# Five x tiles turned by DMA transpose in a transformer block kernel, with weight rows moved and some weight lows on VectorE

## The chip, the core and the metric

The kernel runs on one NeuronCore of a Trainium2 chip. The metric is the device time in microseconds of one execution. The core has TensorE (PE, with its weight loads as PEld), VectorE (DVE), ScalarE (ACT), GpSimd (POOL) and the queue of SyncE (SP), from which nearly all DMAs of this kernel are issued. Each engine works through its own instructions in program order, and waits on semaphores for the others.

## What is computed

One pre-norm block on x of 2048 x 512, in float32: a layer norm, a sliding and dilated attention of 32 heads (8 positions, every second one), an output product with a residual, a second layer norm, and a dense part with squared relu.

```python
x = A_x
h = x + _A_ref(_layernorm(x), A_wqkv, A_wo)     # qkv, local attention, wo
h2 = h + _B_ref(_layernorm(h), B_w1, B_b1, B_w2, B_b2)
# _B_ref: r = relu(x @ w1 + b1); (r * r) @ w2 + b2
```

Float32 precision is kept on TensorE by writing each operand as a sum of a high part (a rounded float32r copy) and a low part (the rest), and by three matmul passes: high by high, low by high, high by low.

## The kernel before

The 2048 rows are 16 tiles of 128 rows. The instruction order of every engine is written out by hand: the program goes through numbered slots, and chores are hung on a slot. At the end of a slot (`end_slot`), the list `due` is run first (`at`), then the attention stream is pumped until its counted VectorE time (`now["dve"]`) has reached the counted TensorE time (`now["pe"]`), then the list `late` is run (`after`). So a chore given to `at` stands ahead of the slot's attention work in the queues of all engines, and one given to `after` stands behind it.

- **Opening** (lines 977 to 1002): 16 slots `n`, qkv products of tiles 0 to 3 by four column groups. Products go in turn to four PSUM banks.
- **First phases** (`first_phase(t0)`, lines 1007 to 1049, for t0 = 4, 6, ..., 14): each does the qkv products of tiles t0 and t0+1, three each, taken in turn (tile t0 first, then t0+1). There are 12 half slots `m`, two to a product; the slot ends in the middle of a product and after it. `evac` (ScalarE, line 523) of a product stands one slot after its end, so that of a phase's last product stands in the `due` list of slot m = 0 of the next phase, ahead of that slot's own chores. In slot 0 and in slot 2 come the statistics (`x_stats`, from tile 6 on ScalarE: `act_stats`, lines 182 to 184, with a finish on POOL) of tiles t0+2 and t0+3, then their norms (`x_norm`), and at m = 9 and 11 (7 and 8 where t0 is 12) their turns `x_T` on TensorE: four transposes into PSUM, a high part by ScalarE, a low part by VectorE (`lo_T`, in `late`). The product takes its passes in the order high by high, xh by the weights' low part, and xl last, so that xh is needed at its start and xl after two thirds of it.
- **Weight jobs** (`weight_job`, line 570): a row of `wo` or `w1` is loaded, and five slots later split: high on ScalarE, low on POOL. Twenty jobs go at m = 0, 3, 6, 9 of the phases 4 to 12.
- **Dense part**: four groups `u` of four tiles. While u = 0 runs (its body is at lines 1087 to 1162), the attention stream is still under way, and the 14 rows of `w2` are split (`split_w2`), low parts on POOL.
- **Attention stream**: multiplications and reductions on VectorE (lines 339, 350, 373) from windows loaded by SP (`load_window`, line 247, two buffers for k and two for v), and three additions on POOL for each step (line 407).
- **A turn by DMA** is already there for twelve o tiles and eight h tiles: `turn_split` (line 616, ScalarE) writes a tile as two planes of 16-bit halves, `turn_dma` (line 620) issues a DMA transpose from SP, and `turn_join` (line 625, ScalarE) puts the halves together again.

All row buffers (x tiles, their parts, raw weights, planes, h) come in rotation from one pool of 15.

Of the kernel before, what the change touches and what calls it, by code (L numbers as in the profile page):

```python
# [9 lines left out]
F32R = mybir.dt.float32r  # L10
# [6 lines left out]
P = 128  # L17
KB = D // P
FB = F // P
R = 4  # L20
# [15 lines left out]
SLOW = 1.01, 1.08, 1.05  # L36
DELAY = 3
WJ = 2
XT = (9, 11), (7, 8)
OT = 4, 5, 10, 12  # L40
WO = 7, 9, 13, 15
HT = 20, 20, 21, 23
# [10 lines left out]
HOLD = 1.0  # L53
XS = 6
WARM = 18


@with_exitstack
def block_kernel(ctx, tc, x, wqkv, wo, w1, b1, w2, b2, out):
    nc = tc.nc  # L60
# [39 lines left out]
    w2_h, w2_l = {}, {}  # L100

    def row(name, shape=(P, D), dt=F32):
        return work.tile(list(shape), dt, name=name, tag="row", bufs=ROWS)
# [9 lines left out]
    def at(delta, fn, *a):  # L113
        due.setdefault(now["slot"] + delta, []).append((fn, a))

    def after(delta, fn, *a):
        late.setdefault(now["slot"] + delta, []).append((fn, a))
# [18 lines left out]
    def dve(t):  # L136
        now["dve"] += t
# [13 lines left out]
    def hi(dst, src):  # L151
        nc.scalar.copy(dst, src)  # L152
# [45 lines left out]
    def transposes(src, banks="tr"):  # L198
        tr = turn[banks].tile("tr").rearrange("p (k c) -> p k c", k=KB)
        for k in range(KB):  # L200
            nc.tensor.transpose(tr[:, k, :], src[:, k * P:(k + 1) * P], ident)  # L201
        now["pe"] += 0.44
        return tr

    def parts(tr, dst):
        n = len(dst)
        return [(dst[i], tr[:, i * KB // n:(i + 1) * KB // n]) for i in range(n)]

    def hi_T(tr, h_dst):
        for d, src in parts(tr, h_dst):  # L210
            hi(d, src)
# [220 lines left out]
    xt, xT = {}, {}  # L432
# [35 lines left out]
    def x_T(t):  # L468
        tr = transposes(xt.pop(t))
        xT[t] = row("xh", (P, KB, P), F32R), row("xl", (P, KB, P), F32R)  # L470
        at(0, hi_T, tr, [xT[t][0]])
        after(0, lo_T, tr, [xT[t][0]], [xT[t][1]])

    ny = [0]

    turn["mm"] = Turn("mm0", "mm1", "acc0", "acc1")
# [63 lines left out]
    def qkv(t, gp, mid=None):  # L540

        ps = turn["mm"].tile("mm")
        xh, xl = xT[t]
        mm3(ps[:, :3 * GP], lambda k: xh[:, k, :], lambda k: xl[:, k, :],
            lambda k: pair(wq_h, k, gp), lambda k: pair(wq_l, k, gp), mid, lows_last=t > 0)
        at(1, evac, t, gp, None, ps)
# [20 lines left out]
    jobs = [(wo_h, wo_l, wo, k, 0, D) for k in range(KB)]  # L567
    jobs += [(w1_h, w1_l, w1, k, c * 448, 448) for k in range(KB) for c in range(4)]

    def weight_job():  # L570
        h, l, src, k, c0, cn = jobs.pop(0)
        raw = row("raw")
        nc.sync.dma_start(raw[:, :cn], src[k * P:(k + 1) * P, c0:c0 + cn])

        def split():
            hi(h[:, k, c0:c0 + cn], raw[:, :cn])
            after(0, lo, nc.gpsimd, l[:, k, c0:c0 + cn], raw[:, :cn], h[:, k, c0:c0 + cn])
        at(5, split)


    hs, hn = {}, {}
# [23 lines left out]
    planes = {}  # L605

    def halves_of(a):
        return a.bitcast(U16).rearrange("p (n two) -> p two n", two=2)

    def two_planes(a):  # L610
        return a.bitcast(U16).rearrange("p (two n) -> p two n", two=2)

    def turn_split(key, src):

        planes[key] = src, row("pl")
        nc.scalar.copy(two_planes(planes[key][1]), halves_of(src))
# [6 lines left out]
    def turn_join(key):  # L623
        src, pl = planes[key]
        nc.scalar.copy(halves_of(pl).rearrange("p two n -> p n two"),
                       two_planes(src).rearrange("p two n -> p n two"))
        planes[key] = pl.rearrange("p (k c) -> p k c", k=KB)
# [317 lines left out]
    warm = turn["tr"].tile("tr").rearrange("p (k c) -> p k c", k=KB)  # L945
    for n in range(WARM):
        nc.tensor.transpose(warm[:, n % KB, :], ident, ident)

    def start_T(t):
        x_T(t)  # L950
        run(due)
        run(late)
# [24 lines left out]
    for n in range(16):  # L977
        gp, t = divmod(n, 4)
        qkv(t, gp, (lambda: start_T(t + 1)) if n < 3 else None)
        if n == 0:  # L980
            x_rstd(2)
            x_center(3)
        if n == 1:
            x_rstd(3)
        if n < 6:
            for k in (0, 1):
                at(0, hi_wqkv, n // 2 + 1, n % 2 * 2 + k)
                after(0, lo_wqkv, n // 2 + 1, n % 2 * 2 + k,
                      nc.gpsimd if k or n < 2 else nc.vector)
        if n == 1:  # L990
            load_wqkv(3)
        if n == 13:
            consts()
        if n in (5, 6, 12, 14):
            at(0, load_x, n - 1 if n < 7 else n // 2)
        if n in (8, 9):
            at(0, x_stats, n - 4)
        if n in (11, 12):
            at(0, x_norm, n - 7)
        if n in (13, 14):  # L1000
            x_T(n - 9)
        end_slot(2.09)
# [4 lines left out]
    def first_phase(t0):  # L1007
        def chores(m):
            if t0 + 3 < 16:
                if m in (0, 2):  # L1010
                    at(0, x_stats, t0 + 2 + m // 2)

                early = t0 == 12
                if m + early in ((4, 6) if t0 == R else (6, 7)):
                    at(0, x_norm, t0 + 2 + (m + early) // 7 if t0 > R else t0 + m // 2)
                if m in XT[early]:
                    x_T(t0 + 2 + XT[early].index(m))
            if t0 + 5 < 16 and m in (6, 9):
                at(0, load_x, t0 + 2 + m // 3)
            if jobs and m % 3 == 0:  # L1020
                at(0, weight_job)
            k = t0 // 2 * 12 - 72 + m
            if k == 19:
                dve(HOLD)
            for t in range(R):
                if k == OT[t]:
                    at(0, load_h, t)
                    o_T(t)
                if t in HV and k == HK[t][0]:
                    at(0, h_split, t)  # L1030
                    after(0, turn_dma, ("h", t))
                if t in HV and k == HK[t][1]:
                    at(0, turn_join, ("h", t))
                if k == WO[t]:
                    wo_product(t, (1, 3, 4, 6))
                    now["pe"] += 2.73
                if k == HT[t]:
                    (at(0, h_parts, t) if t in HV else h_T(t))
            if k in W2:
                at(0, load_w2, W2.index(k))  # L1040

        def half(m):
            end_slot(1.37)
            chores(m)

        for n in range(6):
            chores(2 * n)
            qkv_of(t0 + n % 2, n // 2, lambda: half(2 * n + 1))
            end_slot(1.37)
# [19 lines left out]
    def split_w2(f):  # L1069
        raw = raws.pop(f)  # L1070
        hi(w2_h[f], raw)
        if f < 12:
            place[f] = free.pop(0)
            w2_l[f] = big_l[:, place[f]]
            at(1, stash, f)
        after(0, lo, nc.gpsimd, w2_l[f], raw, w2_h[f])

    def stash(f):
        nc.sync.dma_start(w2l_d[f], w2_l[f].bitcast(F32))
# [7 lines left out]
    for u in range(R - 1):  # L1087
# [11 lines left out]
        for i in js:  # L1099
            t = R * (u + 1) + i  # L1100
# [32 lines left out]
        for p in range(FB + LAG):  # L1133
# [17 lines left out]
            if q >= 0:  # L1151
                f = fs[q]
# [93 lines left out]
```

## Time and profile before

| | us |
|---|---|
| median of 3 runs | 510.53 (510.51 to 511.3) |
| profiled execution, its time | 510.24 |
| its span | 508.5 |

The profile is of one execution. Its times are microseconds from the span's start. In a timeline row stand the start, the duration, the engine, the line, the operation, what it writes and reads, and in brackets the idle time of that engine before it with what ended it. In a row of a group stand the busy time in all, the mean in ns of one, and the idle time before. The starts of the phases on TensorE are at 43.68 (t0 = 4), 61.76 (6), 79.64 (8), 96.92 (10), 114.21 (12) and 138.76 (14); u = 0 runs from 161.60 to about 254.

### The profile page before, as it was taken

Reading aid. Unit: us, or ns where it says so; the run is one execution under the profiler, and the core shown is the slowest. Engines: PE = TensorE matmul, PEld = TensorE weight load, DVE = VectorE, ACT = ScalarE, POOL = GpSimd, SP = SyncE. Lnnn points to the kernel's source line nnn. Section 1 sums busy time; section 2 is a strip of 40 time slices with the busy share of each in tenths; the row PEclk is TensorE's granted clock in tenths of the full one; section 3 lists DMA queues with packets and bytes.
Section 4 is the critical chain, followed back from the end, with each engine's and each line's share of the span. In section 5 each row is a group of like instructions: output and inputs, shape, how many; then the busy total and the mean of one; then the engine's idle time right before and its main releaser. Section 6 shows DMA issues by size and latency. Waiting matters only on the chain.

```text
span 508.5 us, 7542 instructions
## 1 busy us (share of the span) xinstructions
PE 498.6 (98%) x2422; PEld 420.5 (83%) x2422; DVE 375.2 (74%) x507; ACT 305.3 (60%) x558; POOL 361.4 (71%) x439
## 2 busy tenths in 40 slices
PE   8999999999999999999899999999999999999997
PEld 7998778888888887787688888888888888998986
DVE  6479899999999778986898989988951137732233
ACT  4635687577447747478454548756457847566541
POOL 5714789895776999989959777977896364685610
PEclk9999999999999999999999999999999999999999
DMA  8678889899698799789576756997572272444212
GB/s 271 189 212 204 245 290 302 245 307 303 201 228 253 253 273 278 215 216 291 166 248 207 216 147 165 257 252 244 161 173 63 80 212 83 169 123 144 64 43 83
DMA packets 109359, 102.61 MB, mean 202 GB/s; under 512 B 29448, under 2 KB 77832, under 8 KB 109320
## 3 DMA queue, kind: packets, MB, share of 16 engines
q1 hardware_dynamic: 108376, 101.61, 68.0%
q10 hardware_dynamic: 944, 0.52, 0.3%
q8 instruction: 19, 0.31, 0.2%
q14 instruction: 20, 0.16, 0.1%
HBM read 72.65 MB, written 24.25 MB: 191 GB/s over the span
## 4 chain that ended last, share of the span: by engine, by line
PE 66%; POOL 14%; DVE 2%; issue 2%; DMA 2%; ACT 1%; SPq 0%; POOLq 0%; ACTq 0%; DVEq 0%
PE mm L228 30%; PE acc L895 22%; PE wo L228 6%; PE mm L818 6%; POOL pr L407 5%; POOL rl L155 3%; POOL big_l L155 3%; PE tr L201 2%; POOL h L674 1%; DVE pr L350 1%; DMA q<-qkv_d 1%; DMA k<-qkv_d 1%; POOL o L407 1%; POOL w_x L155 1%; POOL rs L171 0%
## 5 line engine op out<-in xcount | busy, mean ns | idle before, releaser
L407 POOL TENSOR_TENSOR pr<-pr 128x512 f32<-128x512 f32 (+1 forms) x128 | 132.3, 1034 | 38.2 <-DVE pr L350 32.7
L228 PE MATMUL mm<-big_l,w_h 128*128 128x512 f32 x336 | 88.9, 391 | 0.7 <-ACT r L871 0.7
L350 DVE TENSOR_TENSOR pr<-ex,v 128x1024 f32<-128x1024 f32 x64 | 78.1, 1221 | 13.5 <-POOL o L407 10.1
L339 DVE TENSOR_TENSOR pr<-qp,k 128x1024 f32<-128x1024 f32 x64 | 76.8, 1200 | 9.3 <-ACT qp L268 8.4
L373 DVE TENSOR_REDUCE ex<-pr 128x64 f32<-128x1024 f32 x64 | 78.5, 1227 | 2.0
L228 PEld LDWEIGHTS mm<-big_l,w_h 128*128 128x128 f32 x336 | 62.8, 188 | 15.0 <-ACT r L871 2.0
L155 POOL TENSOR_TENSOR rl<-r,rh 128x512 fp32r<-128x512 f32 x42 | 55.6, 1326 | 14.9 <-ACT rh L152 14.9
L228 PE MATMUL mm<-big_l,xh 128*128 128x512 f32 (+1 forms) x208 | 55.8, 378 | 0.0
L228 PE MATMUL mm<-big_h,xh 128*128 128x512 f32 (+1 forms) x208 | 53.8, 379 | 1.3 <-ACT xh L152 1.3
L228 PE MATMUL mm<-big_h,xl 128*128 128x512 f32 (+1 forms) x208 | 52.7, 375 | 0.1
L895 PE MATMUL acc<-big_l,rh 128*128 128x512 f32 x190 | 52.2, 390 | 0.0
L895 PE MATMUL acc<-big_h,rh 128*128 128x512 f32 x190 | 52.1, 391 | 0.0
L895 PE MATMUL acc<-big_h,rl 128*128 128x512 f32 x190 | 51.7, 389 | 0.0
L871 ACT ACTIVATE r<-mm,b_sb 128x512 f32<-128x512 f32 x42 | 28.8, 685 | 33.6 <-PE mm L228 30.3
L228 PE MATMUL mm<-big_l,w_l 128*128 128x512 f32 x168 | 44.9, 389 | 0.0
L228 PEld LDWEIGHTS mm<-big_h,xh 128*128 128x128 f32 x208 | 37.6, 188 | 8.6 <-ACT xh L152 3.0
L228 PEld LDWEIGHTS mm<-big_h,xl 128*128 128x128 f32 x208 | 38.2, 188 | 6.4 <-DVE xl L155 0.5
L895 PEld LDWEIGHTS acc<-big_h,rl 128*128 128x128 f32 x190 | 35.7, 188 | 7.4
L895 PEld LDWEIGHTS acc<-big_l,rh 128*128 128x128 f32 x190 | 35.5, 188 | 7.4
L228 PEld LDWEIGHTS mm<-big_l,xh 128*128 128x128 f32 x208 | 37.5, 188 | 4.9
L895 PEld LDWEIGHTS acc<-big_h,rh 128*128 128x128 f32 x190 | 34.9, 188 | 6.7
L228 PEld LDWEIGHTS mm<-big_l,w_l 128*128 128x128 f32 x168 | 31.5, 188 | 6.6
(165 smaller groups left out, 917.8 us busy)
## 6 DMA issues: line engine op xcount, KB each, us to landing
k<-qkv_d SPq DMA_DIRECT2D x48, 288.0 KB, 3.1
v<-qkv_d SPq DMA_DIRECT2D x48, 288.0 KB, 3.6
qkv_d<-y SPq DMA_DIRECT2D x18, 512.0 KB, 5.1
big_l<-w2l_d SPq DMA_DIRECT2D x24, 256.0 KB, 3.1
xt<-in_A_x_dram SPq DMA_DIRECT2D x16, 256.0 KB, 4.7
q<-qkv_d SPq DMA_DIRECT2D x32, 128.0 KB, 3.7
h<-in_A_x_dram SPq DMA_DIRECT2D x16, 256.0 KB, 3.3
h_d<-h SPq DMA_DIRECT2D x16, 256.0 KB, 3.8
```

What stands on the lines that cost most here:

```text
L155: eng.tensor_tensor(out=dst, in0=src, in1=h, op=ALU.subtract)
L201: nc.tensor.transpose(tr[:, k, :], src[:, k * P:(k + 1) * P], ident)
L228: nc.tensor.matmul(ps, l(k), r(k), start=(n == 0), stop=(n == 3 * KB - 1))
L339: nc.vector.tensor_tensor(out=pr.rearrange("p i w h d -> p i w (h d)"), in0=qps["now"][:, j % 2].unsqueeze(2).to_broadcast([P, RI, W, GC]) ...
L350: nc.vector.tensor_tensor(out=p2, in1=vwin, op=ALU.mult, in0=e1[:, :, :, j * GH:(j + 1) * GH].unsqueeze(4).to_broadcast([P, RI, W, GH, DH]))
L373: nc.vector.tensor_reduce(out=lf[:, :, :, j * GH:(j + 1) * GH], in_=pr, axis=X, op=ALU.add)
L407: nc.gpsimd.tensor_tensor(out=dst, in0=p2[:, :, :w], in1=p2[:, :, w:2 * w], op=ALU.add)
L674: nc.gpsimd.tensor_tensor(out=h, in0=h, in1=b2_sb, op=ALU.add)
L818: nc.tensor.matmul(ps, sta[y][:, k], mov[x][:, k], start=(first and q == 0), stop=(last and q == len(terms) - 1), skip_group_check=True)
L871: nc.scalar.activation(r, ps, AF.Relu, bias=b1_sb[:, f:f + 1])
L895: nc.tensor.matmul(acc[j], l[:, j * P:(j + 1) * P], w[f], start=(first and n < len(js)), stop=(last and n >= len(terms) - len(js)))
```

## The change

1. In each phase with t0 up to 12 only the even tile t0+2 is turned on TensorE. The odd tile t0+3 (tiles 7, 9, 11, 13, 15) is split into planes in slot m = 8 (7 where t0 is 12), its DMA transpose stands in that slot's `late` list, and its join with the high and the low part (`x_join`) stands in the `due` list of slot m = 0 of the next phase, behind the statistics of that slot; for tile 15 in slot 11 of phase 12.
2. Weight jobs: three stand in the opening (n = 4, 6, 8), three in each phase up to 12 (m = 0, 4, 8), and the last two in phase 14 (m = 0 and 3). Their splits stand in `late`, four slots on for those of the opening and five for the others, and no longer in `due`.
3. The lows of the second weights' rows 1, 4, 7, 10 and 13 are made by VectorE in place of POOL, with 0.8 us each in the count that paces the attention stream.

```diff
-XT = (9, 11), (7, 8)
+XT = (9,), (7,)
+JOBS = 4, 6, 8
+JM = 0, 4, 8
...
+    def x_split(t):
+        turn_split(("x", t), xt.pop(t))
+
+    def x_join(t):
+        turn_join(("x", t))
+        tr = planes.pop(("x", t))
+        xT[t] = row("xh", (P, KB, P), F32R), row("xl", (P, KB, P), F32R)
+        hi_T(tr, [xT[t][0]])
+        after(0, lo_T, tr, [xT[t][0]], [xT[t][1]])
...
-    def weight_job():
+    def weight_job(delay=5):
...
-        at(5, split)
+        after(delay, split)
...
+        if n in JOBS:
+            at(0, weight_job, 4)
...
-                    x_T(t0 + 2 + XT[early].index(m))
+                    x_T(t0 + 2)
+                if m == 8 - early:
+                    at(0, x_split, t0 + 3)
+                    after(0, turn_dma, ("x", t0 + 3))
+            if m == 0 and R < t0 < 14:
+                at(0, x_join, t0 + 1)
+            if m == 11 and t0 == 12:
+                at(0, x_join, 15)
...
-            if jobs and m % 3 == 0:
+            if jobs and m in (JM if t0 < 14 else (0, 3, 5)):
...
-        after(0, lo, nc.gpsimd, w2_l[f], raw, w2_h[f])
+        eng = nc.vector if f % 3 == 1 else nc.gpsimd
+        after(0, lo, eng, w2_l[f], raw, w2_h[f])
+        if eng is nc.vector:
+            dve(0.8)
```

## The prediction

> **What bounds the kernel now.** Read first the page's busy shares, then who made TensorE wait, then the busy times by stage (each window, its length, then PE, PEld, DVE, ACT and POOL busy, the granted clock, the DMA share).
>
> ```profile
> span 508.5 us, 7542 instructions
> PE 498.6 (98%) x2422; PEld 420.5 (83%) x2422; DVE 375.2 (74%) x507; ACT 305.3 (60%) x558; POOL 361.4 (71%) x439
> ...
> PE tr L201 <- ACT hn L196: 1.4, 1, 1.4
> ...
> PE mm L228 <- ACT xh L152: 1.3, 2, 0.7
> PE wo L228 <- DVE ol L155: 0.8, 1, 0.8
> PE mm L228 <- ACT r L871: 0.7, 1, 0.7
> ...
> 96.00:113.00 17.00, 17.00 (x80) 14.10 (x79) 16.34 (x23) 11.65 (x27) 14.84 (x21) 1.00 0.92 276
> ...
> 164.00:190.00 26.00, 26.00 (x117) 21.52 (x116) 20.04 (x22) 16.02 (x27) 24.89 (x26) 1.00 0.81 254
> ...
> 215.00:240.00 25.00, 24.20 (x104) 19.29 (x104) 19.74 (x25) 19.45 (x29) 22.57 (x27) 1.00 0.93 240
> 240.00:255.00 15.00, 13.55 (x63) 10.76 (x62) 13.17 (x21) 7.73 (x17) 13.67 (x17) 1.00 0.62 187
> ```
>
> TensorE has hardly an idle moment: in the first phases (96 to 113) it is busy throughout, so whatever is taken from it or makes it wait there goes straight into the time. The waits of 0.8, 0.7 and 1.4 us (on `ol`, `r` and `hn`, all between 200 and 254) lie in the first group of the dense part. There POOL is busy 24.89 of 26 us and 13.67 of 15, and the wait for `hn` comes down from POOL's statistics:
>
> ```profile
> 251.07 0.61 POOL rs L171
> ...
> 252.08 0.82 ACT hn L196
> ```
>
> So two stages matter: TensorE sets the pace up to 161 us, and from there to 254 POOL's backlog costs it 0.8 + 0.7 + 1.4 = 2.9 us.
>
> **The turns taken from TensorE.** In the timeline of PE, a product without a turn and one with a turn in it:
>
> ```profile
> 96.92 1.09 PE L228 MATMUL mm<-big_h,xh 128*128 128x512 f32 x4
> ...
> 99.66 1.07 PE L228 MATMUL mm<-big_h,xh 128*128 128x512 f32 x4
> ...
> 107.82 1.07 PE L228 MATMUL mm<-big_h,xh 128*128 128x512 f32 x4
> 108.73 0.62 PE L228 MATMUL mm<-big_l,xh 128*128 128x512 f32 x2
> 109.19 0.60 PE L201 MATMUL tr<-ident,xt 128*128 128x128 f32 x4
> ...
> 111.02 1.07 PE L228 MATMUL mm<-big_h,xh 128*128 128x512 f32 x4
> ```
>
> A product takes 99.66 - 96.92 = 2.74 us, one with four transposes 111.02 - 107.82 = 3.20. A turn costs 0.46 us, and five fewer give 5 x 0.46 = **-2.3 us**. Nothing covers TensorE here, so all of it counts.
>
> **The splits at slot ends.** TensorE, ScalarE and the end of phase 4:
>
> ```profile
> 60.07 1.09 PE L228 MATMUL mm<-big_h,xl 128*128 128x512 f32 x4
> 61.76 1.20 PE L228 MATMUL mm<-big_h,xh 128*128 128x512 f32 x4 [0.60 <-ACT xh L152]
> 62.80 1.08 PE L228 MATMUL mm<-big_l,xh 128*128 128x512 f32 x4
> ...
> 64.00 1.20 PE L228 MATMUL mm<-big_h,xl 128*128 128x512 f32 x4
> ...
> 60.12 0.62 ACT L152 CAST wo_h<-raw 128x512 fp32r<-128x512 f32 x1 [2.35 <-DMA raw<-in_A_wo_dram]
> ```
>
> Four matmuls follow one another in 108.73 - 107.82 = 0.91 us. The last four of phase 4 would free the array at 60.98, and phase 6 starts at 61.76; its xl matmuls start at 64.00 where 62.80 + 0.91 = 63.71 was possible. That is 0.78 + 0.29 = 1.07 us lost, because ScalarE waited 2.35 us for a raw weight row ahead of the high part of tile 6. With the split in `late` and the jobs at other slots, that high part stands ahead of the wait: **-1.1 us** (0 if the raw row is late at another place).
>
> **The joins.** This is the term that decides. The odd tile is needed by the second product of a phase, 2.74 us after the phase's start. Its join stands in ScalarE's queue behind the evacuation of the last product of the phase before, which cannot start until that product is done, and behind a whole set of ScalarE statistics. Both are in the trace at the start of phase 10 (96.92), and a join with its high part, from an o tile, below them:
>
> ```profile
> 97.18 0.59 ACT L523 COPY y<-mm 128x512 f32<-128x512 f32 x1 [0.74 <-PE mm L228]
> ...
> 99.28 0.19 ACT L184 ACTIVATION_READ_ACCUMULATOR scrap<-xt,nm 128x1 f32 x1
> ...
> 237.78 1.16 ACT L625 COPY pl<-o 128x1024 uint16<-128x1024 uint16 x1
> 238.97 0.62 ACT L152 CAST oh<-pl 128x512 fp32r<-128x512 f32 x1
> ```
>
> The statistics end at 99.28 + 0.19 = 99.47. The join takes 238.97 - 237.78 = 1.19 to its reader's start, the high part 0.62: 101.28. The product could have started at 99.66. TensorE, in order, waits 1.6 us with nothing else to do, in each of the phases 6, 8, 10 and 12: 4 x 1.6 = **+6.4 us**. Tile 15, joined a slot before its phase, has time. The low part on VectorE stands behind the high part; xl is needed 2 x 0.91 us into the product, more than the 0.84 us of such a subtraction (row further down), so it adds nothing unless VectorE is late itself.
>
> The join also needs its DMA. What the trace says of such transposes, of a load for comparison (the last number is its median time to landing), of a transpose that was waited for, and of the place in SP's queue:
>
> ```profile
> L620 SPq DMA_TRANSPOSE o<-pl x12: 1237/1238/4488, 195.4 to 392.4; - x12
> DMA to landing us min/median/max: 3.5/6.3/7.0
> ...
> k<-qkv_d SPq DMA_DIRECT2D x48, 288.0 KB, 3.1
> ...
> 202.34 1.24 SPq L620 DMA_TRANSPOSE o<-pl  x1
> ...
> 205.98 1.18 ACT L625 COPY pl<-o 128x1024 uint16<-128x1024 uint16 x1 [0.90 <-DMA o<-pl]
> ...
> 59.42 1.16 DVE L339 TENSOR_TENSOR pr<-qp,k 128x1024 f32<-128x1024 f32 x1
> ...
> 61.71 0.53 SPq L247 DMA_DIRECT2D k<-qkv_d  x1
> ...
> 78.16 0.49 SPq L438 DMA_DIRECT2D xt<-in_A_x_dram  x1
> ```
>
> From issue to landing: 205.98 - 202.34 = 3.6 us where the join waited, 3.5 to 7.0 in the recorded ones. With the DMA share of 0.92 in phase 10 I take 4.5, nearer to the low end, where the wait was seen. In phase 4 the transpose stands behind the k load of 61.71, which overwrites a window that VectorE reads until 59.42 + 1.16 = 60.58. With 0.5 us for that load it issues at 61.1 and lands at 65.6; join and high part end at 65.6 + 1.8 = 67.4. The product would start at 60.98 - 0.46 + 2.74 = 63.3: a wait of 4.1 us, 2.5 over the 1.6. VectorE may be a little earlier with fewer loads queued, so I take **+2.0 us** (0 if VectorE and SP run 2 us earlier; 61.1 + 7.0 + 1.8 gives 69.9 and 5.0). In phase 6 the transpose stands just ahead of the load at 78.16; phase 8 would then start near 60.5 + 16.8 + 3.6 = 80.9 (six products of 2.74 and one turn are 16.9), and a landing at 82.7 lies ahead of the statistics' end 2.55 us after the start: 0, at worst (7.0) 1.7. Later phases start 1.6 us later each while VectorE, whose loads SP waits for, keeps its pace: 0.
>
> [...]
>
> **The lows on VectorE, and POOL's relief.**
>
> ```profile
> L155 POOL TENSOR_TENSOR big_l<-raw,big_h 128x512 fp32r<-128x512 f32 x12 | 15.6, 1298 | 0.0
> L155 DVE TENSOR_TENSOR rl<-r,rh 128x512 fp32r<-128x512 f32 x14 | 11.7, 836 | 22.5 <-ACT rh L152 21.2 <-POOL traw L788 1.4
> ```
>
> POOL loses 5 x 1.30 = 6.5 us in a stage in which it cost TensorE 2.9; VectorE gets 5 x 0.84 = 4.2 us where it has 26 - 20.04 = 6 us free from 164 to 190. TensorE also arrives later, so the attention stream has more of its work behind it. I take **-2.7 us** of the 2.9. The other end: the low waits on VectorE for ScalarE's high part, and the stream queued behind it (its multiplications, and POOL's additions after them) waits too; then 0, or a loss of about 1 us.
>
> **The three rows in the opening.** The highs of two of them (0.62 us each, as at 60.12) come on ScalarE ahead of the norm of tile 4, and their loads run beside a store that ScalarE waits for already:
>
> ```profile
> 32.95 1.05 ACT L521 ACTIVATE y<-mm,rs 128x384 f32<-128x384 f32 x2 [5.96 <-DMA qkv_d<-y]
> ...
> 36.80 0.80 ACT L196 ACTIVATE xt<-xt,rs 128x512 f32<-128x512 f32 x1
> ...
> 38.63 0.60 PE L201 MATMUL tr<-ident,xt 128*128 128x128 f32 x4
> ```
>
> The norm ends at 37.60, the turn needs it at 38.63: 1.03 us of slack against 1.24 and a slower store. **+0.4 us**, between 0 and 1.5. Their lows find POOL waiting for work. At nothing I cost the last two rows in phase 14 (used by the eighth product of the dense part, some 30 us on), the issues of 1.24 us on SP and the splits on ScalarE (in the trace ScalarE has 17 - 11.65 = 5 us free in a phase, behind the products' own waits); without that cover each would add its own microsecond to a phase.
>
> **Sum**, against the profiled execution's 510.24: -2.3 - 1.1 + 6.4 + 2.0 - 2.7 + 0.4 = +2.7, so 512.9. The median of the runs shown stands 0.29 above that execution: **513.2**.
>
> **Rivals.**
> - *Joins in time* (faster). If ScalarE has the odd tile's high part ready within 2.74 us of a phase's start, the 8.4 us fall away: 510.5 - 2.3 - 1.1 - 2.7 + 0.4 = 504.8. It decides at that point: evacuation, statistics, join and high part in 2.74 us. Against it stand the rows at 97.18 and 99.28, which leave 0.2 us for 1.8; for it, that the same join is in use for twenty tiles, though with two slots of lead.
> - *Only the floor* (no change): 6.4 for the joins, landings never late, the opening free and all 2.9 regained: 510.5 - 2.3 - 1.1 + 6.4 - 2.9 = 510.6. For it: the transpose of phase 4 may go out earlier, since ScalarE's wait up to 60.12 held back what stood behind it, for other engines too.
> - *No relief in the dense part*: VectorE's lows hold up the stream and the 2.9 stay with 1 more: 513.2 + 2.7 + 1.0 = 516.9. For it: VectorE's 6 us without work there are no free time if they are waits in its order already; against: POOL's 6.5 us.
> - *Late landings in two phases*: +3.0 in phase 6 and +1.7 in phase 8 beyond the sum: 517.9.
>
> **How the numbers follow.** The forecast with its own range of 511.6 to 515.5 has 0.58, joins in time 0.11, the floor 0.14, no relief 0.10, two late landings 0.07. The forecast's bounds are those of the +2.0 (0 to 5) and of the 0.4, not all at once. The range goes from 510.2, just under the floor, to 516.9; joins in time and the last case lie outside. Within 0.2% (1.0 us, about what a measurement tells from no change) lies the floor: faster 0.11, same 0.15, slower 0.74.
>
> **What would show it.** After: PE's waits for `xh` at the second product of phases 6 to 12, some 1.6 us each, the first longer; on ScalarE the order evacuation, statistics, join, high part at those places; sixteen less five turns of x; no wait before phase 6's first product; waits between 200 and 254 near 0 and POOL's busy share there down by 6.5 us. I am wrong if those waits for `xh` are missing, or if the waits from 164 to 254 add up to more than before.

## The result and the profile after

| | before | after |
|---|---|---|
| median, us | 510.7 (510.51 to 511.3, 4 runs) | 528.51 (527.92 to 529.4, 4 runs) |
| ratio after to before | | 1.0351 [1.0328, 1.0374] |
| profiled execution, its time | 510.24 | 528.4 |
| its span | 508.5 | 526.5 |

The change makes the kernel 17.8 us slower, where 2.7 were forecast. From the page of the changed kernel (line numbers of the shared helpers are two higher than before):

```profile
span 526.5 us, 7513 instructions
PE 501.5 (95%) x2402; PEld 423.5 (80%) x2402; DVE 378.0 (72%) x512; ACT 315.0 (60%) x568; POOL 356.5 (68%) x434
```

TensorE has twenty matmuls fewer (five turns of four) and yet is busy 2.9 us longer, and it stands still 15 us more. Its waits in the changed kernel (who waited for whom: us in all, times, the longest):

```profile
PE mm L230 <- ACT xh L154: 10.3, 5, 5.3
PE wo L230 <- ACT ohl L154: 5.9, 2, 4.3
PE mm L230 <- ACT r L883: 1.5, 1, 1.5
...
PE tr L203 <- ACT hn L198: 1.3, 1, 1.3
PE mm L230 <- DVE xl L157: 0.7, 1, 0.7
```

The waits for `xh` are the ones that the prediction named. The waits for `ohl` and `r` lie in the dense part, where it saw a gain. The timeline of the changed kernel (start, duration, engine, line, operation, in brackets the wait before it and its end) around both, in chosen rows:

```profile
60.87 1.16 DVE L341 TENSOR_TENSOR pr<-qp,k 128x1024 f32<-128x1024 f32 x1
...
62.06 0.97 SPq L249 DMA_DIRECT2D k<-qkv_d  x1
62.80 1.07 PE L230 MATMUL mm<-big_h,xh 128*128 128x512 f32 x4
63.31 3.44 SPq L632 DMA_TRANSPOSE xt<-pl  x1
...
66.44 0.58 ACT L535 COPY y<-mm 128x512 f32<-128x512 f32 x1
68.54 0.19 ACT L186 ACTIVATION_READ_ACCUMULATOR scrap<-xt,nm 128x1 f32 x1
70.11 1.16 ACT L637 COPY pl<-xt 128x1024 uint16<-128x1024 uint16 x1 [1.39 <-DMA xt<-pl]
71.30 0.62 ACT L154 CAST xh<-pl 128x512 fp32r<-128x512 f32 x1
71.97 2.08 PE L230 MATMUL mm<-big_h,xh 128*128 128x512 f32 x4 [5.32 <-ACT xh L154]
72.01 0.69 DVE L157 TENSOR_TENSOR xl<-pl,xh 128x512 fp32r<-128x512 f32 x1 [4.61 <-ACT xh L154]
73.84 1.91 PE L230 MATMUL mm<-big_l,xh 128*128 128x512 f32 x4
...
92.24 0.98 PE L230 MATMUL mm<-big_h,xh 128*128 128x512 f32 x3 [1.42 <-ACT xh L154]
...
231.34 1.05 ACT L628 COPY pl<-o 128x1024 uint16<-128x1024 uint16 x1 [8.10 <-POOL o L409]
...
238.44 2.11 POOL L409 TENSOR_TENSOR pr<-pr 128x512 f32<-128x512 f32 x2 [1.25 <-DVE pr L352]
241.05 1.28 POOL L157 TENSOR_TENSOR big_l<-raw,big_h 128x512 fp32r<-128x512 f32 x1
242.36 0.69 ACT L883 ACTIVATE r<-mm,b_sb 128x512 f32<-128x512 f32 x1 [3.41 <-POOL big_l L157]
244.26 1.15 ACT L637 COPY pl<-o 128x1024 uint16<-128x1024 uint16 x1
245.45 0.62 ACT L154 CAST ohl<-pl 128x512 fp32r<-128x512 f32 x1
246.12 1.88 PE L230 MATMUL wo<-wo_h,ohl 128*128 128x512 f32 x4 [4.34 <-ACT ohl L154]
```

Three things are to be seen. First, phase 6 starts at 62.80 without a wait, and its second product, on tile 7, stands 5.32 us behind the transposing DMA that went out at 63.31 and let ScalarE on at 70.11. Second, the four matmuls at 71.97 take 2.08 us, those at 73.84 take 1.91, where such four take about 1.07. Third, in the dense part ScalarE stands 8.10 us ahead of a split, because POOL's addition of the attention stream comes late, and later 3.41 us ahead of `r`, behind a low of POOL. The windows of the changed kernel (window, its length, then PE, PEld, DVE, ACT and POOL busy, the granted clock, the DMA share) show the slow matmuls as a halved clock, and the last one gives POOL's share in the dense part:

```profile
60.00:72.00 12.00, 6.00 (x26) 4.29 (x25) 7.21 (x11) 6.70 (x14) 9.53 (x14) 0.87 1.14 324
72.00:76.00 4.00, 4.00 (x10) 3.22 (x11) 3.96 (x6) 2.69 (x8) 2.08 (x4) 0.54 0.37 121
76.00:80.00 4.00, 4.00 (x20) 3.26 (x19) 3.79 (x6) 1.55 (x4) 1.79 (x2) 1.00 0.50 146
...
246.00:250.00 4.00, 3.88 (x10) 3.10 (x11) 3.08 (x4) 3.94 (x8) 0.07 (x1) 0.57 0.19 54
...
212.00:266.00 54.00, 49.66 (x214) 40.49 (x212) 41.07 (x53) 30.73 (x49) 42.00 (x48) 0.97 0.75 205
```

**Where the 18 us went.** The timelines of PE give the start of each product, before and after. The difference of the two (after less before) at the start of each stretch grows as follows; a stretch's own cost is the growth over it. The forecast's terms are put in the same stretches, a turn of 0.46 us taken off where it was.

| stretch | start before | start after | lag at its end | its own cost | forecast |
|---|---|---|---|---|---|
| opening | | | +2.26 | +2.26 | +0.4 |
| phase 4 | 43.68 | 45.94 | +1.04 | -1.22 | -1.5 |
| phase 6 | 61.76 | 62.80 | +8.30 | +7.26 | +3.1 |
| phases 8 and 10 | 79.64 | 87.93 | +10.81 | +2.51 | +2.3 |
| phase 12 | 114.21 | 125.02 | +12.00 | +1.19 | +1.1 |
| phase 14 | 138.76 | 150.76 | +12.00 | 0 | 0 |
| dense part, to the last matmul | 161.60 | 173.60 | +18.15 | +6.15 | -2.7 |
| sum | | | | +18.15 | +2.7 |

Two stretches hold nearly all of the error: the dense part (8.8 us off, with the sign wrong) and phase 6 (4.1 off). The opening adds 1.9, of which 1.4 arise in its first product.

### The profile page after: what moved, and what is told of

It reads as the page before. It is cut to its first block, busy times and chain, and to the rows that moved or that the text cites. A ratio compares the mean times of both kernels' runs of the same rounds, so it can differ in the third digit from the quotient of the medians.

```text
span 526.5 us, 7513 instructions
## 1 busy us (share of the span) xinstructions
PE 501.5 (95%) x2402; PEld 423.5 (80%) x2402; DVE 378.0 (72%) x512; ACT 315.0 (60%) x568; POOL 356.5 (68%) x434
## 5 line engine op out<-in xcount | busy, mean ns | idle before, releaser
L230 PE MATMUL mm<-big_h,xh 128*128 128x512 f32 (+1 forms) x208 | 55.3, 389 | 10.3 <-ACT xh L154 10.3
L230 PEld LDWEIGHTS mm<-big_l,xh 128*128 128x128 f32 x208 | 38.6, 192 | 5.4
L535 ACT COPY y<-mm 128x512 f32<-128x512 f32 x36 | 21.1, 585 | 33.0 <-PE mm L230 27.6
```

The costliest lines, as they stand in the source:

```text
L230: nc.tensor.matmul(ps, l(k), r(k), start=(n == 0), stop=(n == 3 * KB - 1))
```

## The experiments

Each kernel is given as an edit of the changed kernel or of the kernel before. The runs of before that each is compared with had medians of 510.0 to 510.3 us. The theory after the result: the turns cost by late landings and joins, and the rest by what these do to the attention stream. The rivals: the moved weight rows, or the lows on VectorE, are what costs.

### Taking the change apart

**e1: the odd tiles turned on TensorE again**, the rest as changed.

```diff
-XT = (9,), (7,)
+XT = (9, 11), (7, 8)
...
-                if m == 8 - early:
-                    at(0, x_split, t0 + 3)
-                    after(0, turn_dma, ("x", t0 + 3))
-            if m == 0 and R < t0 < 14:
-                at(0, x_join, t0 + 1)
-            if m == 11 and t0 == 12:
-                at(0, x_join, 15)
```

> The changed kernel with its odd x tiles turned on TensorE again; jobs and lows stay as changed. Theory J (the place of the joins: TensorE waits for xh at four phase starts, VectorE stands behind the same high parts with the attention stream queued after it, and that lag comes back as waits for ohl in the dense part) expects 508 to 512 us, no wait for xh at the second product of phases 6 to 12, and the waits for ohl (4.3, 1.6 and 1.5 us in the changed kernel) gone. Theory P (the five lows on VectorE and the 0.8 us each in the pacing count put the stream behind in the dense part) expects those three waits to stay: about 518 to 520 us. Theory D (DMA transposes slow the other loads) expects what J expects.

Measured: 514.28 us, ratio 1.0076 [1.0053, 1.01], between the ranges of the theories. The waits on `ohl` fall under 0.6 us each, which theory J has and theory P hasn't. So the turns carry 14 of the 18 us, and the other two parts together cost about 4 where the forecast had a gain of 3.4.

**e2: the lows of the second weights on POOL again**, the rest as changed.

```diff
-        eng = nc.vector if f % 3 == 1 else nc.gpsimd
+        eng = nc.gpsimd
```

> The changed kernel with all lows of the second weights on POOL again, and without their 0.8 us in the pacing count. Theory J expects little: 526 to 530 us, with the waits at the phase starts unchanged. Theory P expects the waits for ohl gone: about 519 us.

Measured: 525.14 us, 1.0285 [1.0242, 1.0328], just under theory J's range; of the waits on `ohl` one of 1.80 is left. The lows on VectorE make the changed kernel slower by 3.4, not faster by 2.7. Note that with them goes their count of 0.8 us each.

**e5: the moved weight rows alone** (before, with rows in the opening, at other slots, and late splits; as e1 and e2 together).

> The kernel before with the moved weight jobs and their splits at slot ends alone. The prediction's own terms (-1.1 for the wait of phase 6, +0.4 in the opening) expect 509 to 510 us. The rival, that the loads in the opening and the splits behind the attention work cost more than they give (opening waits of 0.6 and 1.2 us on TensorE were seen with the turns back on TensorE), expects 511 to 513 us.

Measured: 513.54 us, 1.0063 [1.0045, 1.0082], just over the rival's range. The wait ahead of phase 6 is gone, as forecast, but the opening is 2.5 us later at phase 4's start, and a wait comes at 164. There VectorE's four subtractions take 4.29 us, 1.07 each (timeline of e5):

```profile
158.93 4.29 DVE L157 TENSOR_TENSOR big_l<-pl,big_l 128x256 fp32r<-128x256 f32 x4 [1.05 <-ACT big_l L154]
```

Before, the same four took 2.9 us in all. POOL works on a late weight row's low beside them in e5 (161.59, 1.34 us); whether that is the reason was not separated.

**e6: the lows on VectorE alone** (before, with the edit of `split_w2` only).

> The kernel before with the five lows on VectorE alone. The prediction's relief of POOL expects 507 to 508.5 us, with the waits of 0.8, 0.7 and 1.4 us near 0. The rival, that the lows and their 0.8 us in the count put the attention stream back, expects 511 to 514 us, with new waits for ohl near 235 and 325 and ScalarE waiting for POOL's o ahead of its splits.

Measured: 509.53 us, 0.9979 [0.9961, 0.9997], between the two ranges. The gain is about 0.6 us, against the forecast's 2.7: the wait of 0.8 goes, that of 1.4 falls to 0.7, that of 0.7 on `r` stays, and new ones of 0.5, 0.6 and 0.9 come after 320.

**e16: the turns by DMA alone** (before, with `x_split`, `x_join` and the turns' slots; weight rows and lows as before).

> The kernel before with nothing but the turns by DMA of tiles 7, 9, 11, 13 and 15 (weight rows at the old slots with splits in due, all lows on POOL). Theory A (the turns cost the same whatever stands beside them; 525.14 - 513.54 = 11.6 beside the moved rows): 521 to 523. Theory B (the moved rows put VectorE and so the transpose of phase 4 back, and the wait in phase 6 is short without them): 516 to 519, with a first wait on xh of under 3 us and no half clock behind it.

Measured: 521.79 us, 1.0236 [1.0216, 1.0255]: +11.8, inside theory A's range, and the wait on tile 7 was 3.04, just over theory B's limit. Its timeline:

```profile
62.79 2.88 SPq L632 DMA_TRANSPOSE xt<-pl  x1
...
63.16 1.63 PE L230 MATMUL mm<-big_h,xh 128*128 128x512 f32 x4 [2.40 <-ACT xh L154]
...
70.81 2.08 PE L230 MATMUL mm<-big_h,xh 128*128 128x512 f32 x4 [3.04 <-ACT xh L154]
```

Both waits, 2.40 and 3.04, are followed by slow matmuls, 1.63 and 2.08 us for four, with a granted clock of 0.59 from 63 to 67 and 0.57 from 70 to 74. The turns cost 11.8 by themselves, the rows 3.4, the lows -0.6; the three together cost 17.8, which is 3.2 more than their sum of 14.6. In e16 the dense part adds only 0.8 us to the lag that it starts with (10.5 to 11.3), in e1 1.8, in the changed kernel 6.15: most of the dense part's loss belongs to no part alone.

### The late landing in phase 6

**e3: the join ahead of the statistics in slot 0.**

```diff
+            if m == 0 and R < t0 < 14:
+                at(0, x_join, t0 + 1)
             if t0 + 3 < 16:
...
-            if m == 0 and R < t0 < 14:
-                at(0, x_join, t0 + 1)
```

> The changed kernel with the join ahead of the statistics in the slot m = 0. Theory J expects the 1.42 us at phases 8, 10 and 12 to fall to 0, since 2 us of statistics are no longer ahead of the join, and phase 6, whose join waits for its transpose to land at 70.1, to keep about 5 us: 521 to 525 us. Theory D expects the landings to be the bound everywhere, so that the joins wait for the DMA in place of the statistics and no more than 1 us is gained.

Measured: 527.31 us, 1.0346 [1.0317, 1.0375]: 1.2 us gained, nearest to theory D. In phase 6 ScalarE simply waits for the landing (3.15 us), and TensorE still 4.97; in phases 8 and 12 its wait falls from 1.42 to about 0.8, in phase 10 it rises to 1.68. With the statistics behind them, the joins stand 1.0, 1.9 and 1.0 us for their landings in phases 8, 10 and 12, so the statistics were not all that they waited for.

**e4: every join at slot 11 of the phase in which the tile was split.**

```diff
-            if m == 0 and R < t0 < 14:
-                at(0, x_join, t0 + 1)
-            if m == 11 and t0 == 12:
-                at(0, x_join, 15)
+            if m == 11 and t0 + 3 < 16:
+                at(0, x_join, t0 + 3)
```

> The changed kernel with every join in slot m = 11 of the phase of its split, as tile 15 has it. Theory J expects ScalarE to have xh ready before the phase start from phase 8 on, VectorE not to stand behind it, and the waits for ohl to shrink with the lag: 512 to 518 us, with a wait left in phase 6, where the transpose lands late. Theory P expects the waits for ohl to stay: 519 to 521 us. Theory D expects ScalarE to stand waiting for landings, three slots after the split, and the time to stay above 522.

Measured: 533.68 us, 1.0466 [1.044, 1.0492], in theory D's range. TensorE waits 5.10, 1.24, 4.73 and 1.34 us. Its timeline:

```profile
62.24 3.36 SPq L632 DMA_TRANSPOSE xt<-pl  x1
...
69.03 1.16 ACT L637 COPY pl<-xt 128x1024 uint16<-128x1024 uint16 x1 [6.18 <-DMA xt<-pl]
```

The DMA lands 6.8 us after its issue, and ScalarE stands before it with all that is queued behind. An earlier place in the order gains nothing: what is late is the landing.

**e8: the DMA issued in `due`, ahead of the slot's loads.**

```diff
-                    after(0, turn_dma, ("x", t0 + 3))
+                    at(0, turn_dma, ("x", t0 + 3))
```

> The changed kernel with the DMA transpose ahead of the slot's k, v and q loads in SP's queue. If the place behind the k load is what makes the landing of tile 7 late (issued at 63.3, 2.6 us after its planes are written at 60.7, landed at 70.1), the wait of 5.3 us in phase 6 falls to 2 to 3 us, the half clock behind it goes, and the time falls by 3 to 5 us, to 523.5 to 525.5. If the transfer itself is slow under load, it stays at 527 to 529.

Measured: 526.77 us, 1.0313 [1.0277, 1.0348], between the two ranges. Its timeline:

```profile
60.62 1.71 SPq L632 DMA_TRANSPOSE xt<-pl  x1
...
65.96 0.58 ACT L535 COPY y<-mm 128x512 f32<-128x512 f32 x1
...
69.99 1.22 PE L230 MATMUL mm<-big_h,xh 128*128 128x512 f32 x2 [3.42 <-ACT xh L154]
```

With the issue 2.7 us earlier the join waits for no landing any more, and 1.9 us of TensorE's wait are gone. The rest, 3.42, is ScalarE, which waited 2.18 for the load of `q` ahead of the evacuation at 65.96. The slow matmuls stay, two in 1.22 us where two take 0.62 at full clock.

**e9: tile 7 alone on TensorE.**

```diff
+                if t0 == R and m == 11:
+                    x_T(t0 + 3)
-                if m == 8 - early:
+                if m == 8 - early and t0 > R:
...
-            if m == 0 and R < t0 < 14:
+            if m == 0 and R + 2 < t0 < 14:
```

> The changed kernel with tile 7 alone on TensorE again (tiles 9, 11, 13 and 15 by DMA). If the wait of phase 6 belongs to tile 7 and the late opening (5.3 us and 1.9 us of half clock behind it, less 0.46 for the turn), the time falls by 6 to 7 us, to 521 to 523, and 1.4 us each stay at phases 8, 10 and 12. If it only moves on to tile 9, phase 8 shows 4 to 5 us and the time stays above 526.

Measured: 521.6 us, 1.0239 [1.0207, 1.0272], 6.9 less than the changed kernel and in the first range. Phase 6 costs nothing now, but the first tile that is turned by DMA, tile 9, waits 3.24 in place of 1.42, with a granted clock of 0.50 from 86 to 90 (timeline of e9):

```profile
86.97 2.07 PE L230 MATMUL mm<-big_h,xh 128*128 128x512 f32 x4 [3.24 <-ACT xh L154]
```

In the changed kernel TensorE comes to phase 8 7.1 us later (87.93 against 80.85), and waits 1.42 there; a wait removed at one tile is in part found again at the next. The dense part adds 3.0 in place of 6.15.

**e17: no weight rows in the opening**, five in phase 14 for the two.

```diff
-        if n in JOBS:
-            at(0, weight_job, 4)
...
-            if jobs and m in (JM if t0 < 14 else (0, 3, 5)):
+            if jobs and m in (JM if t0 < 14 else (0, 2, 3, 4, 5)):
```

> The changed kernel without the three weight rows in the opening; those that are left over go to phase 14, five in place of two (m = 0, 2, 3, 4, 5). Theory A (the opening is late by its rows and costs by itself about 1.5 us, and the wait in phase 6 does not hang on it): 526 to 527.5, the wait in phase 6 near 5 us as before. Theory B (the rows of the opening make the attention stream start late, and the wait in phase 6 and those of the dense part with it): under 524.

Measured: 536.83 us, 1.0529 [1.0507, 1.0552], slower than either theory had it. The opening is clean (the lag at phase 4's start is 1.62, all but 0.04 of it from the first product) and the wait on tile 7 is 5.19 all the same, so it doesn't hang on the rows of the opening. But the five rows in phase 14 cost 8.6 us of their own up to the dense part's start (timeline of e17):

```profile
169.81 0.81 ACT L198 ACTIVATE hn<-h,rs 128x512 f32<-128x512 f32 x1 [8.03 <-DMA h_d<-h]
...
170.68 0.82 PE L203 MATMUL tr<-ident,hn 128*128 128x128 f32 x4 [2.95 <-ACT hn L198]
...
181.17 1.10 PE L230 MATMUL mm<-big_l,w_h 128*128 128x512 f32 x2 [3.67 <-DVE big_l L157]
```

The two of the change were hidden there; five are not.

**e18: idle matmuls in the wait on tile 7.** They multiply tile 6's high part by a weight row into the bank that the next product overwrites.

```diff
+        if (t, c) == (7, 0):
+            for _ in range(22):
+                nc.tensor.matmul(ps, xT[6][0][:, 0, :], wq_h[:, 0, cs], start=True, stop=True)
```

> The changed kernel with 22 idle matmuls (tile 6's high part by a weight row, into the bank that the next product overwrites) ahead of tile 7's first product, so that TensorE works through most of its wait of 5.3 us in phase 6. Theory A (the clock falls to a half because TensorE stood still for so long, and the matmuls behind the wait run at half speed for that): the granted clock stays at 1.0 from 64 to 85 us, the first groups of four behind the wait take about 1.07 us in place of 2.08, and the time falls by 1.5 to 2 us to 526.5 to 527. Theory B (the clock falls for another reason, or the matmuls behind the wait are slow by their operands): no change, 528 to 529.

Measured: 528.41 us (five runs: 526.15, 526.41, 528.41, 528.58, 528.89), 1.0355 [1.0335, 1.0376]: by the median theory B's number. The profiled execution (526.15) has the product behind the wait at full speed. Its timeline:

```profile
65.84 5.15 PE L549 MATMUL mm<-big_h,xh 128*128 128x512 f32 x22
71.02 1.20 PE L230 MATMUL mm<-big_h,xh 128*128 128x512 f32 x4
```

And its window of the same 4 us that had the halved clock in the changed kernel:

```profile
72.00:76.00 4.00, 4.00 (x19) 3.27 (x19) 3.86 (x7) 2.79 (x8) 1.79 (x4) 1.00 0.21 70
```

The clock is 1.00 where it was 0.54, with the same operands and the join let on by its landing at 69.15 (70.11 in the changed kernel): TensorE's standing still is what halved it, as theory A has it. In that execution phase 8 starts with a lag of 5.61 in place of 8.30, 0.3 of the 2.7 us coming from an earlier phase 6; 0.6 is lost again at tile 9, which then waits 2.01 us in place of 1.42. The five runs fall into two groups some 2.3 us apart, and why is open; so the mechanism is shown, in one profiled execution, and its worth in the median is not.

### The dense part

**e7: the join's low part a slot later**, so that VectorE shouldn't stand behind the high part.

```diff
-        after(0, lo_T, tr, [xT[t][0]], [xT[t][1]])
+        after(1, lo_T, tr, [xT[t][0]], [xT[t][1]])
```

> The changed kernel with the low part of a joined tile one slot later in VectorE's order, so that the attention work of that slot stands ahead of it. If VectorE's standing behind the high part (15.6 us before xl in all) feeds the lag of the dense part, the waits for ohl shrink and the time falls by 2 to 5 us, to 523 to 526. If the lag comes from the jobs and lows, the time stays at 527 to 529, or grows by a wait for xl at the phase starts.

Measured: 534.07 us, 1.0458 [1.0423, 1.0494]: neither of the outcomes put down, but slower. New waits of 1.79 and 2.13 us come at 174 and 178, with four matmuls in 1.80 us behind the second; ScalarE stands 3.4 us behind a late `xl`. The edit brought a wait of its own, so it says nothing on VectorE's standing.

**e11: a turn by DMA counted as one on TensorE.** The attention stream is pumped until its counted time reaches TensorE's; `transposes` counts 0.44 us, `x_split` nothing.

```diff
         turn_split(("x", t), xt.pop(t))
+        now["pe"] += 0.44
```

> The changed kernel with 0.44 us put on the counted TensorE time at each split of an x tile, so that the attention stream is pumped as far ahead as with the turns on TensorE. If the lower count (2.2 us in all) is what puts the stream behind and makes the waits for ohl, the time falls by 2 to 5 us, to 523.5 to 526.5. If the lag is from engines that stand waiting, it stays within 1.5 us of 528.

Measured: 526.17 us, 1.0317 [1.0291, 1.0343], in the first range. After 240 no wait is over 0.92 us; but the wait on tile 13 is 3.12 in place of 1.42.

**e12: the lows on VectorE, not counted.**

```diff
-        if eng is nc.vector:
-            dve(0.8)
```

> The changed kernel with the five lows on VectorE but without their 0.8 us each in the count. With the lows back on POOL the time was 525.1. If the count is what costs the 3 us, this kernel is at 524.5 to 526; if VectorE's work or its waits for the high parts do, it stays at 527 to 529.

Measured: 524.83 us, 1.0294 [1.027, 1.0318], the same as with the lows on POOL (e2, 525.14). So it is the count of 0.8 us that costs 3.7, not VectorE's work. In e12's timeline the split that waited 8.10 us waits 7.14, its join stands behind its transpose alone, and TensorE waits 1.76 in place of 4.34, with the clock left at 1.0:

```profile
230.07 1.05 ACT L628 COPY pl<-o 128x1024 uint16<-128x1024 uint16 x1 [7.14 <-POOL o L409]
...
241.18 1.17 ACT L637 COPY pl<-o 128x1024 uint16<-128x1024 uint16 x1 [1.17 <-DMA o<-pl]
...
243.05 1.21 PE L230 MATMUL wo<-wo_h,ohl 128*128 128x512 f32 x4 [1.76 <-ACT ohl L154]
```

Not all of it is gained: a wait of 1.90 on the low part of a weight row (`big_l`) comes at 265, and the mean granted clock of that execution is 0.990, where one stretch of 6.8 us at half clock, as in phase 6 of the changed kernel, would leave 0.993.

**e15: both counts**, the edits of e11 and e12 together.

> The changed kernel with both alterations of the attention stream's count at once: 0.44 us of TensorE's time counted for each turn by DMA as for a turn on TensorE, and nothing counted on VectorE's side for a low of the second weights. Theory A (the counts put the stream back, and nothing else in the dense part does): the waits of TensorE on ohl and hn after 240 us, 4.3 and 1.3 us, fall under 0.7 each, no half clock there, but the waits at tiles 9 to 13 and the first one stay or grow: 522 to 525. Theory B (VectorE's own standing behind the high parts of the joins, 15.6 us in all, puts the stream back whatever is counted): a wait of over 1.5 us on ohl stays, 525 to 528.

Measured: 526.81 us, 1.0332 [1.0313, 1.0351]. The wait on `ohl` is gone, as theory A has it, but not that on `hn`, and the time is in theory B's range. The stream now runs ahead: no split of an o tile there waits over 1.2 us, but TensorE waits 2.53 on tile 13, 1.60 and 1.40 on `oh` and `ol` at 218 and 222, and 1.75 on `hn`. So the counts place the loss; no setting of them removes it.

### A version of the parts that cost nothing

**e13: before, with the lows on VectorE, the splits in `late` at the old slots, and tile 15 alone by DMA.**

```diff
-        at(5, split)
+        after(5, split)
...
-                if m in XT[early]:
+                if m in XT[early] and t0 + 2 + XT[early].index(m) < 15:
                     x_T(t0 + 2 + XT[early].index(m))
+                if early and m == 7:
+                    at(0, x_split, 15)
+                    after(0, turn_dma, ("x", 15))
+                if early and m == 11:
+                    at(0, x_join, 15)
```

> The kernel before with those parts alone that cost nothing where they were seen: the five lows on VectorE, the splits in the late list at the old jobs' places, and the DMA turn of tile 15 alone (joined a slot before its phase). If the parts add up (-0.6 for the lows, about -0.7 for the wait ahead of phase 6, -0.46 for the turn), it is at 508.3 to 509 us, faster than both kernels by more than the bound of 0.2 percent. If they disturb one another as the three parts of the change did, it is at 510 to 512.

Measured: 509.86 us, 0.9984 [0.9968, 1.0], just under the second range. One of its twelve executions took 1013.9 us, and why is open; the others took 507.72 to 511.27. It is the only one with a turn by DMA that isn't slower; its gain (0.4 us between the medians) is at the edge of what can be told. At its dense part's start it is 0.5 us ahead of before, a turn's worth.

## Why the prediction was wrong

That the kernel becomes slower was forecast, and the joins cost what they were forecast to cost. What was missed are 15 of the 18 us: the size of one landing with what follows it, and the dense part, where a gain became a loss.

**Turns off TensorE (-2.3) and the wait ahead of phase 6 (-1.1): right.** TensorE has twenty matmuls fewer, phase 4 is 1.22 us shorter where 1.5 were forecast, and no wait stands before 62.80.

**Joins (4 x 1.6): right in size, and in mechanism for a part.** Phases 8, 10 and 12 wait 1.42 us each. Their stretches of 2.51 and 1.19 us are within 0.2 of the forecast. But the forecast put the landings of these phases at nothing, and the statistics weren't the whole reason: where the join goes ahead of them (e3), the landing is nearly as late.

**The late landing in phase 6 (+2.0): the mechanism right, the size wrong.** The stretch costs 7.26, the forecast 3.1. Of its working two steps failed, and two more were not in it.

The issue was put at 61.1 and came at 63.31. The k load ahead of it waits for VectorE, whose multiplication ended at 60.87 + 1.16 = 62.03 and not at 60.58, and that load held SP for 0.97 us in place of 0.5.

The landing was put 4.5 us on, "nearer to the low end, where the wait was seen"; ScalarE was let on at 70.11, 6.8 us on, the upper end. The low end was that of the o tiles' transposes in the dense part. What goes out at the place of tile 7's transpose lands later, whether it transposes or not (issues with KB each and the median us to landing, where it is recorded). In the kernel before, from 56 to 64 us:

```profile
k<-qkv_d SPq DMA_DIRECT2D x2, 352.0 KB, 7.1
...
raw<-in_A_wo_dram SPq DMA_DIRECT2D x2, 256.0 KB, 7.0
```

In the changed kernel, from 58 to 72:

```profile
k<-qkv_d SPq DMA_DIRECT2D x2, 352.0 KB, 7.1
...
xt<-pl SPq DMA_TRANSPOSE x1, 6.8
```

Plain loads took 7 us here before the change already. The 3.1 us of the k loads in the prediction is a median over the whole page, and hid that. The DMA engines' share was full at this time (1.14 from 60 to 72 in the changed kernel), and the issue alone held SP for 3.44 us against the 1.24 of the forecast (duration on SP in ns of the transposes of x in the changed kernel: least, median, most):

```profile
L632 SPq DMA_TRANSPOSE xt<-pl x5: 1247/1973/3445, 63.3 to 142.9; - x5
```

Not in the forecast at all was that the long wait would cost twice. Behind 5.32 us the granted clock was 0.50 (up to 75.7), and the product took 76.55 - 71.97 = 4.58 us in place of 2.74, another 1.8. The e18 run shows the cause. A wait of 0.69 for tile 6's `xl`, at 65.46, came on top. So of the 4.1 us by which the stretch was off, the longer wait makes 1.7 (5.32 against 1.6 + 2.0), the clock 1.8 and the `xl` 0.7. The prediction's case of a landing at 7.0 us had priced only the wait.

**POOL's relief (-2.7): wrong, with the sign.** The step that failed is "POOL loses 5 x 1.30 = 6.5 us in a stage in which it cost TensorE 2.9". POOL did lose it. From 200 to 254 it was busy 50.17 of 54 us before (the row below, in the order of the windows above), and 42.00 in the same stretch after (212 to 266):

```profile
200.00:254.00 54.00, 50.77 (x221) 39.88 (x220) 45.48 (x58) 35.31 (x58) 50.17 (x57) 1.00 0.82 225
```

But its own work was not what was late in the changed kernel; its additions at 238.44 stand 1.25 us for VectorE. The waits of TensorE there come to 4.3 + 1.3, with two more of 1.5 later. A full POOL did not by itself cost TensorE anything here: the prediction's row from 164 to 190 has POOL busy 24.89 of 26 us, and TensorE 26.00. Nor were all 2.9 us POOL's to give back: in e6, with five lows fewer on POOL, the wait on `r` stays at 0.7.

The forecast costed the 0.84 us of work of a low, but not the diff's `dve(0.8)`. That count, and the 0.44 that no longer counts on TensorE's side, decide how far the attention stream is pumped: five lows counted at 0.8 hold back 4.0 us of it by the count, five turns not counted another 2.2. In the changed kernel POOL's low at 241.05 then stands behind the stream's additions, `r` at 242.36 stands 3.41 us behind that low, and the join of an o tile at 244.26 behind `r`. The wait of 3.41 is what tells the kernels apart. It is in the changed kernel and in e3, e4, e7, e8, e17 and e18, which share both counts and all five turns, and in all seven TensorE waits 3.99 to 4.34 us on `ohl`. In all others `r` waits at most 0.3 us for such a low: where no low is counted (e2, e5, e12, e15, e16), where all turns are on TensorE or counted as if they were (e1, e6, e11), and where fewer tiles are turned by DMA (e9, e13). The split that waits 8.10 us at 231.34 does not tell them apart, since e1, e2, e6, e12 and e16 have such a wait of 7.1.

The e12 run takes the count of the lows away and gives 3.7 us back; VectorE's own work costs nothing that can be told (e12 against e2). The rival "no relief in the dense part" had the right direction, and its "loss of about 1 us" was too small. Where the turns are counted, the lows with the same count do no harm: e6, the edit alone on the kernel before, gains 0.6.

**VectorE behind the high part: the condition was met.** The text had it that the low part "adds nothing unless VectorE is late itself". By the groups of the changed kernel (busy in all, mean ns, then the idle time before):

```profile
L157 DVE TENSOR_TENSOR xl<-pl,xh 128x512 fp32r<-128x512 f32 x5 | 4.9, 979 | 12.2 <-ACT xh L154 12.2
L157 DVE TENSOR_TENSOR big_l<-raw,big_h 128x512 fp32r<-128x512 f32 x4 | 5.0, 1249 | 0.0
```

VectorE stood 12.2 us behind five high parts, and the attention stream is queued behind it. Four of the five lows took 1.25 us on the mean, not 0.84; the fifth, on another tile, 0.68. How much of the dense part's loss comes from this standing was not settled: e7, made for it, brought a wait of its own, and e15 still loses 16.8 with the counts set back.

**The opening (+0.4, bound 1.5): too small in most executions.** Without the rows it costs 0.04 (e17), with them 0.3 to 2.8 in the profiled executions: the lag at phase 4's start less that in the first product is 2.26 - 1.44 = 0.8 in the changed kernel and 2.52 - 0.40 = 2.1 in e5. The 1.44 us in the first product belong to no part: the same stretch differs by -0.1 to +1.6 between the executions of kernels that share it.

**The last two rows in phase 14, at nothing: right for two** (the stretch costs 0 in the changed kernel), though e5 then waits 0.92 at 164, and five cost 8.6 (e17).

The two conditions that the prediction named for being wrong: the waits for `xh` were there, but the waits in the first dense group (4.3 + 1.3) came to more than the 2.9 of before. What went wrong beyond sizes is that the terms were added. Each was priced in a trace in which TensorE never waits for more than 1.45 us. The parts measured one by one give 14.6 and together 17.8. The difference arises in the dense part, which in the profiled executions loses 0.8 us with the turns alone (e16), 0.8 with the rows (e5), 0.2 with the lows (e6), and 6.15 with all three.

## What to carry to other kernels

A wait on the engine that sets the pace is priced with what follows it: behind each of the eleven waits of 2.40 to 5.32 us listed below TensorE came back at about half speed, and 5.3 us of waiting cost 7.2. Where an instruction order is written out by a counted time, read every change of the count as a move of work, and ask what is queued behind the piece that moves; before counting on relief for a busy engine, ask whether its inputs are in time (POOL's additions at 238.44 stood 1.25 us for VectorE). Read the landing time of a new DMA from what goes out at the same place, and not from a median over the kernel. And a transposing DMA that replaces 0.46 us of the busiest engine needs here a landing time (6.8 us for tile 7), two copies on ScalarE (1.05 and 1.16 us) and a place in three queues, which only tile 15 had to spare.

## What the runs showed of the hardware

- **The clock behind a wait.** Four matmuls took about 1.07 us at full clock, two 0.62 and three 0.84. Behind the waits of 5.32 and 4.34 us of the changed kernel four took 2.08 and 1.88, and the granted clock was 0.50 from 68.9 to 75.7 and from 246.4 to 249.8 us. Behind 2.40 and 3.04 in e16 four took 1.63 and 2.08, behind 3.24 in e9 and 5.19 in e17 2.07 each; behind 4.97 in e3 and 5.10 in e4 three took 1.65 each; behind 3.42 in e8 and 3.67 in e17 two took 1.22 and 1.10; behind 2.95 in e17 four transposes took 0.82, where four take 0.60, and the next two full groups of four 1.91 and 1.36. Up to 1.79 us nothing of the kind is in these rows: behind 1.42 (three times) in the changed kernel, 1.36 and 1.37 in e16 and 1.76 in e12 four took 1.19 to 1.21, and behind 1.45 in the kernel before and 1.79 in e7 four transposes took 0.66. Between them both are there: behind 2.01 in e18 four took 1.19, behind 2.13 in e7 1.80.
- **Landing late.** From 58 to 72 us, with the DMA engines' share at 1.14 (60 to 72), the k loads of the changed kernel landed in 7.1 us at the median and the transpose in 6.8; over its whole page the k loads of 288 KB have a median of 3.0.
- **Issuing a transpose.** SP was held 1.24 us at the median by the twelve transposes of o tiles in the changed kernel (1.23 to 1.42), and 3.44 us by the one of tile 7 at 63.31; by that of tile 7 2.88 in e16, 3.36 in e4, 1.71 in e8.
- **VectorE's subtractions vary.** The same 128x512 low of a weight row took 1.25 us in the changed kernel and 0.88 in e12 on the mean of four, and 0.68 at the least in the changed kernel. What makes the difference was not separated by any run.
